# Zeros on PE before the first inputs, v scaled on GpSimd ahead of its loads, and k of three batches turned by DMA transposes

One core of a Trainium2 chip. The metric is the device time of one execution in microseconds (us), median over the runs; most runs of one kernel lie within 0.3% to 1% of each other. A run over 1.5% above the fastest of its kernel counts as slow here, and only fast runs are compared.

## The reference

Two stages. A block-wise linear attention with decay over q, k, v of 4 batches x 8 heads x 768 positions x 64; then a token mixer whose input x is the attention's output.

```python
# attention, per head, blocks of 64: rel = i - j
intra = (qb @ kb.T * where(rel >= 0, lam ** rel, 0)) @ vb
inter = (qb * lam ** (pos + 1)) @ kv_state
kv_state = lam ** 64 * kv_state + (kb * lam ** (63 - pos)).T @ vb
out = intra + inter
# mixer, per batch
W = (x @ w_q) @ (x @ w_k).T / sqrt(64)
y = relu(W @ x) @ w_out
```

## The kernel before

PE is the engine for matmuls, DVE the one for vectors, ACT the one for activations, GpSimd (POOL in the views) a general one; SyncE (SP) issues transfers. SBUF is the memory on the chip that they work from, HBM the large one outside it. k turned is kT, v scaled is vn.

The kernel walks over 16 pairs of heads (4 batches x 4 pairs, numbered 0 to 15), with chunks of 128 positions. The decay is folded into q (multiplied by `Dq`) and into v (multiplied by `DvI`). All inputs are float32 in HBM and are cast to bf16 by loads that GpSimd issues, five pairs ahead. For a pair, PE turns q and k (transposes against an identity), makes the scores, the states (`dps`) and the output (`oa`); DVE masks the scores; ACT copies kT and the output. The mixer's matmuls of the batch before are woven between (`pq`, `py`, `pm`, `po`). The instructions of each engine run in program order. The code is shortened; `NP` is 4 (pairs in a batch), `N` 16, and `...` stands for what is left out.

```python
def load_kv(n):                                    # GpSimd: one issue for k, one for v
    for nm, src in (("k", k), ("v", v)):
        t = stage.tile([128, 2, NCH, D], BF16, tag="f" + nm, name="f" + nm)
        nc.gpsimd.dma_start(out=t, in_=kv_rows(n, src))

def turn(n):
    ...                                            # 12 transposes of q, qT on DVE
    trk = pst([128, S], BF16, "trk")
    for c in range(NCH):
        for hl in range(2):
            nc.tensor.transpose(trk[hl*64 : hl*64+64, c*CH : (c+1)*CH], kn[:, hl, c, :], ident)
    nc.scalar.copy(out=kT, in_=trk)

for n in range(N):
    if n + AHEAD < N:
        load(n + AHEAD)                            # q, k, v of pair n + 5
    if n == 0:
        load_wo()
    if n + 2 < N:
        take_k(n + 2)
        if n + 2 >= NP:
            scale_v(n + 2, nc.gpsimd)              # vn = v * DvI, pairs 4 to 15
    scores(n)
    ...                                            # mixer parts of the batch before
    inter(n)
    if n + 2 < NP:
        scale_v(n + 2, nc.vector)                  # pairs 2 and 3
    values(n)
    states(n + 1)                                  # needs vn of pair n + 1
    turn(n + 2)
```

## Time and profile before

| | before |
|---|---|
| time | 109.6 us (109.4 to 109.9) |
| span in the profile | 108.0 us |
| PE, GpSimd, DVE, ACT busy | 88.6, 65.5, 69.3, 65.2 us |
| loads: last packet | 71.6 us |
| loads while undisturbed | some 160 GB/s of bf16, 3.6 us a pair |

The busy shares say that PE is the fullest engine, but they are an average.

One row misleads, as the prediction notes: the page's clock row of this kernel is 9 throughout. The trace's first clock record of this run is at 20.0 us; until then the page shows full speed.

### The profile page before, as it was taken

The page shows a single profiled execution, that of the slowest core. Times are in us where ns is not written, and L with a number is a line of the kernel's source. Part 1 is how long each engine was busy: PE and PEld are TensorE (multiplying, and loading weights), DVE is VectorE, ACT ScalarE, POOL GpSimd, SP SyncE. Part 2 cuts the span into 40 slices and gives each one's busy share as a digit, 9 for nine tenths or more (in the row PEclk, how much of TensorE's full clock was granted, in tenths as well). Part 3 has the DMA queues.
Part 4 walks back from the last instruction along what each step waited for, and adds up shares of the span by engine and source line. Part 5 has one row for each costly group of instructions (what it writes and reads, how often), then busy time and mean ns, then how long its engine had stood idle before and what let it go on. Part 6 is the DMA issues. An engine that isn't in the chain of part 4 may idle for free. (4 is left out here: it accounts for less than half of the span.)

```text
span 108.0 us, 3286 instructions
## 1 busy us (share of the span) xinstructions
PE 88.6 (82%) x1392; PEld 58.7 (54%) x1392; DVE 69.3 (64%) x168; ACT 65.2 (60%) x119; POOL 65.5 (61%) x68
## 2 busy tenths in 40 slices
PE   0013979977796998899999999999999999998950
PEld 0013849666474766657686557487675645543410
DVE  1435597999975979772988918458988190227440
ACT  4036194845547268678665969696488777647420
POOL 5999999849979999999999999232000000000000
PEclk9999999999999999999999999999999999999999
DMA  0999999999999999999999999990000435522383
GB/s 17 187 168 164 165 162 161 167 164 170 197 164 168 163 162 164 164 167 189 251 210 166 166 166 213 263 283 11 6 0 0 178 119 194 194 97 103 142 323 118
DMA packets 67406, 16.93 MB, mean 157 GB/s; under 512 B 63808, under 2 KB 64320, under 8 KB 67392
## 3 DMA queue, kind: packets, MB, share of 16 engines
q0 software_dynamic: 61184, 9.77, 121.6%
q1 hardware_dynamic: 6208, 6.95, 19.3%
q8 instruction: 11, 0.18, 0.6%
q14 instruction: 3, 0.02, 0.1%
HBM read 20.19 MB, written 6.29 MB: 245 GB/s over the span
## 5 line engine op out<-in xcount | busy, mean ns | idle before, releaser
L282 DVE TENSOR_TENSOR pr<-sc,maskc 128x384 bf16<-128x384 f32 x64 | 31.1, 550 | 0.6
L423 PE MATMUL po<-wo,rmT 128*128 128x512 bf16 x96 | 22.3, 379 | 0.0
L322 ACT CAST xT<-oa 128x384 bf16<-128x384 f32 x32 | 17.3, 594 | 5.9 <-PE oa L314 5.1
L193 POOL TENSOR_TENSOR vn<-fv,DvI 128x768 bf16<-128x768 bf16 x12 | 17.8, 1498 | 3.8 <-PE trk L223 3.8
L227 ACT COPY kT<-trk 128x768 bf16<-128x768 bf16 x16 | 12.8, 799 | 10.6 <-PE trk L223 10.2
L434 ACT COPY osb<-po 128x512 f32<-128x512 f32 x21 | 12.3, 586 | 8.8 <-PE po L423 7.2
L77 POOL DMA_DIRECT2D fk<-in_k_dram x15 | 15.8, 1056 | 2.3 <-DMA fq<-in_q_dram 1.6
L77 POOL DMA_DIRECT2D fv<-in_v_dram x15 | 15.6, 1039 | 0.4 <-DMA fq<-in_q_dram 0.3
L208 PE MATMUL trq<-ident,fq 128*64 128x128 bf16 x192 | 9.3, 237 | 7.6 <-DMA fq<-in_q_dram 7.6
L71 POOL DMA_DIRECT2D fq<-in_q_dram x16 | 14.1, 883 | 1.1 <-POOLq L519 0.8
L423 PEld LDWEIGHTS <-rmT 128*128 128x128 bf16 x96 | 9.1, 98 | 9.9 <-DVE rmT L407 0.5
L250 DVE COPY two<-dps 128x64 f32<-128x64 f32 x16 | 3.6, 224 | 16.6 <-PE dps L240 16.6
L314 PE MATMUL oa<-pr,vn 128*64 128x128 bf16 x192 | 10.9, 228 | 2.6 <-DVE pr L282 2.2
L335 DVE COPY xnat<-xp 128x768 bf16<-128x768 bf16 x16 | 8.8, 550 | 4.9 <-PE xp L334 4.9
L270 PE MATMUL sc<-qT,kT 64*128 64x128 bf16 x192 | 10.8, 228 | 0.9 <-ACT kT L227 0.5
L416 ACT ACTIVATE rmT<-pm 128x384 bf16<-128x384 f32 x28 | 11.5, 507 | 0.0
L208 PEld LDWEIGHTS <-fq 128*64 128x64 bf16 x192 | 7.0, 121 | 7.6 <-DMA fq<-in_q_dram 7.6
L214 DVE TENSOR_TENSOR qT<-trq,dq 128x768 bf16<-128x768 bf16 x16 | 8.8, 550 | 2.4 <-PE trq L208 2.4
L314 PEld LDWEIGHTS <-vn 128*64 128x64 bf16 x192 | 7.0, 111 | 5.5 <-issue 4.1
L270 PEld LDWEIGHTS <-kT 64*128 64x128 bf16 x192 | 7.1, 99 | 4.2 <-issue 2.1
L334 PE MATMUL xp<-ident,xT 128*128 128x128 bf16 x96 | 8.4, 225 | 0.3
L223 PE MATMUL trk<-ident,fk 128*64 128x128 bf16 x180 | 8.4, 232 | 0.1
(53 smaller groups left out, 107.3 us busy)
## 6 DMA issues: line engine op xcount, KB each, us to landing
out_dram<-osb SPq DMA_DIRECT2D x24, 256.0 KB, 2.2
fq<-in_q_dram POOLq DMA_DIRECT2D x16, 192.0 KB, 7.5
fv<-in_v_dram POOLq DMA_DIRECT2D x16, 192.0 KB, 8.5
fk<-in_k_dram POOLq DMA_DIRECT2D x15, 192.0 KB, 8.0
wo<-in_moe_w_out_dram POOLq DMA_DIRECT2D x1, 512.0 KB, 11.0
k<-in_k_dram SPq DMA_DIRECT2D x1, 384.0 KB, 3.9
wqk_f<-in_moe_w_q_dram SPq DMA_DIRECT2D x1, 128.0 KB, 5.9
wqk_f<-in_moe_w_k_dram SPq DMA_DIRECT2D x1, 128.0 KB, 7.2
```

What stands on the lines that cost most here:

```text
L71: nc.gpsimd.dma_start(out=t, in_=q_rows(n))
L77: nc.gpsimd.dma_start(out=t, in_=kv_rows(n, src))
L193: eng.tensor_tensor(out=vn, in0=fv, in1=DvI[:, 2 * kk : 2 * kk + 2, :].unsqueeze(3).to_broadcast([128, 2, NCH, D]), op=ALU.mult,)
L208: nc.tensor.transpose(trq[hl * 64 : hl * 64 + 64, a, r, :], fq[:, hl, a, r * D : (r + 1) * D], ident,)
L227: nc.scalar.copy(out=kT, in_=trk)
L270: nc.tensor.matmul(sc[a, hl][:, cc, :], kT[r, c * CH : (c + 1) * CH], qchunk(n, r, c), start=True, stop=True, skip_group_check=True,)
L282: nc.vector.tensor_tensor(out=t, in0=sc[a, hl], in1=maskc, op=ALU.mult)
L314: nc.tensor.matmul(oa[a][r, cc, :], vn[:, hl, c, :], pr[a, hl][:, cc, :], start=False, stop=(cc == 2), skip_group_check=True,)
L322: nc.scalar.copy(out=xT[b][:, kk, a * HALF : (a + 1) * HALF].rearrange("d (c p r) -> d c r p", c=3, r=2), in_=oa[a].rearrange("d c (r p) - ...
L416: nc.scalar.activation(out=to, in_=pms[dd, n], func=ACT.Relu, scale=1.0 / 8.0)
L423: nc.tensor.matmul(po, M[b]["rmT"][:, kt, t * CH : (t + 1) * CH], wo[:, kt, :], start=(kt == 0), stop=(kt == 3),)
L434: nc.scalar.copy(out=osb, in_=po)
```

## The change

Intent: warm PE's clock while it waits for q; stop PE's waits for v by scaling it ahead of the loads in GpSimd's order, and take two more v and four copies off DVE; take 144 transposes off PE and twelve copies off ACT, by letting the DMA engines turn k. The diff is shortened.

```diff
+WARM = 11
 def load_kv(n):
-    for nm, src in (("k", k), ("v", v)):
-        t = stage.tile([128, 2, NCH, D], BF16, tag="f" + nm, name="f" + nm)
-        nc.gpsimd.dma_start(out=t, in_=kv_rows(n, src))
+    t = stage.tile([128, NCH, 2, D], BF16, tag="fk", name="fk")
+    for hl in range(2):
+        nc.gpsimd.dma_start(out=k_rows(t)[:, hl], in_=kv_rows(n, k)[:, hl])
+    t = stage.tile([128, 2, NCH, D], BF16, tag="fv", name="fv")
+    nc.gpsimd.dma_start(out=t, in_=kv_rows(n, v))
 def turn(n):
+    if n >= NP:
+        return                                     # after q's part
+def turn_k(n):
+    kT = tsb.tile([128, S], BF16, tag="kT", name="kT")
+    nc.sync.dma_start_transpose(
+        out=kT.rearrange("d (c p) -> d c p", p=128),
+        in_=L[n]["kn"].rearrange("p c h d -> p (c h d)"),
+    )
 def flip(n):                                       # the xnat copy
+    if b == 0: nc.scalar.copy(...)                 # else nc.vector, as before
+for _ in range(WARM):
+    nc.tensor.matmul(warm, blank[:, 0:128], blank, start=True, stop=True)
 for n in range(N):
+    if n + 2 < N:
+        take_k(n + 2)
+        if n + 2 >= NP:
+            turn_k(n + 2)
+        scale_v(n + 2, nc.gpsimd)                  # pairs 2 to 15
     if n + AHEAD < N:
         load(n + AHEAD)
-    if n + 2 < N: ... scale_v(n + 2, nc.gpsimd)    # was here; pairs 2, 3 on nc.vector below
```

A DMA transpose of a pair wants k with both heads side by side in each chunk. A load that writes this pattern in one issue does not build, so each k load becomes two.

More of the change, by code (lines that the diff above doesn't have):

```diff
@@ L67, in kv_rows, with k_rows @@
         return src[b, 2 * kk : 2 * kk + 2].rearrange("h (c p) d -> p h c d", p=128)
+    def k_rows(t):
+        return t.rearrange("p c h d -> p h c d")
     def load_q(n):
@@ L74, in load_kv @@
     def load_kv(n):
-        for nm, src in (("k", k), ("v", v)):
-            t = stage.tile([128, 2, NCH, D], BF16, tag="f" + nm, name="f" + nm)
-            nc.gpsimd.dma_start(out=t, in_=kv_rows(n, src))
-            staged[n, nm] = t
+        t = stage.tile([128, NCH, 2, D], BF16, tag="fk", name="fk")
+        for hl in range(2):
+            nc.gpsimd.dma_start(out=k_rows(t)[:, hl], in_=kv_rows(n, k)[:, hl])
+        staged[n, "k"] = t
+        t = stage.tile([128, 2, NCH, D], BF16, tag="fv", name="fv")
+        nc.gpsimd.dma_start(out=t, in_=kv_rows(n, v))
+        staged[n, "v"] = t
     def load(n):
@@ L98 @@
     nc.scalar.preload_act_table_set("natural_log_exp_and_others")
+    blank = consts.tile([128, HD], BF16, name="blank")
+    nc.vector.memset(blank, 0.0)
     ident = consts.tile([128, 128], BF16, name="ident")
@@ L182, in take_k @@
         if n == 0:
-            kn = nat.tile([128, 2, NCH, D], BF16, tag="kn", name="kn")
-            nc.vector.tensor_copy(out=kn, in_=k0)
+            kn = nat.tile([128, NCH, 2, D], BF16, tag="kn", name="kn")
+            nc.vector.tensor_copy(out=k_rows(kn), in_=k0)
         else:
@@ L219, in turn @@
         )
+        if n >= NP:
+            L[n].update(qT=qT)
+            return
         trk = pst([128, S], BF16, "trk")
@@ L223, in turn @@
                 nc.tensor.transpose(
-                    trk[hl * 64 : hl * 64 + 64, c * CH : (c + 1) * CH], kn[:, hl, c, :], ident
+                    trk[hl * 64 : hl * 64 + 64, c * CH : (c + 1) * CH], kn[:, c, hl, :], ident
                 )
@@ L228, in turn @@
         L[n].update(qT=qT, kT=kT)
+    def turn_k(n):
[4 more added lines that the diff above has]
+        )
+        L[n]["kT"] = kT
     def qchunk(n, r, c):
@@ L241, in states @@
                     dps[hl * 64 : hl * 64 + 64, c:end, :],
-                    kn[:, hl, c, :],
+                    kn[:, c, hl, :],
                     vn[:, hl, c, :].unsqueeze(1).to_broadcast([128, end - c, D]),
@@ L334, in flip @@
             nc.tensor.transpose(xp[:, t, :], xT[b][:, kk, t * CH : (t + 1) * CH], ident)
-        nc.vector.tensor_copy(out=xnat[b][:, :, kk * CH : (kk + 1) * CH], in_=xp)
+        to = xnat[b][:, :, kk * CH : (kk + 1) * CH]
+        if b == 0:
+            nc.scalar.copy(out=to, in_=xp)
+        else:
+            nc.vector.tensor_copy(out=to, in_=xp)
     M = {}
@@ L435, in mix_po @@
         nc.sync.dma_start(out=out[b, t * CH : (t + 1) * CH, :], in_=osb)
+    warm = pst([128, HD], F32, "warm")
+    for _ in range(WARM):
+        nc.tensor.matmul(warm, blank[:, 0:128], blank, start=True, stop=True)
     make_dq(0)
@@ L456 @@
             load_wo()
-        if n + 2 < N:
-            take_k(n + 2)
-            if n + 2 >= NP:
-                scale_v(n + 2, nc.gpsimd)
         scores(n)
@@ L479 @@
         inter(n)
-        if n + 2 < NP:
-            scale_v(n + 2, nc.vector)
         values(n)
```

## The prediction

> **What bounds the kernel now.** I read the page's busy shares and slices first, then the instructions in order of time on each engine, then the table of waits, then the chain that ended last.
>
> ```profile
> PE   0013979977796998899999999999999999998950
> DVE  1435597999975979772988918458988190227440
> ACT  4036194845547268678665969696488777647420
> POOL 5999999849979999999999999232000000000000
> DMA  0999999999999999999999999990000435522383
> ```
>
> A slice is 2.7 us. PE is full from about 43 us to the end. GpSimd is full nearly from the start to about 67 us, and the DMA engines are full to about 72 us. So there are two regimes: until about 45 us loads and GpSimd pace PE, afterwards PE paces itself. The page's chain (PE 15%, all of it after 86.9 us) speaks only for the tail, so I take the middle from the order of time.
>
> ```profile
> 48.00 0.89 POOL L71 DMA_DIRECT2D fq<-in_q_dram  x1
> 48.88 1.03 POOL L77 DMA_DIRECT2D fk<-in_k_dram  x1
> 49.88 1.05 POOL L77 DMA_DIRECT2D fv<-in_v_dram  x1
> 50.91 1.51 POOL L193 TENSOR_TENSOR vn<-fv,DvI 128x768 bf16<-128x768 bf16 x1
> 52.33 0.89 POOL L71 DMA_DIRECT2D fq<-in_q_dram  x1
> ```
>
> This is one pair of heads on GpSimd (columns: start, duration, both us): 4.33 us from one q issue to the next, back to back. GpSimd has no room here. It stays ahead of PE only because a PE iteration in batches 2 and 3 takes about 5 us (scores of pair 8 at 51.11, of pair 12 at 71.92: 20.8 us for four).
>
> ```profile
> DVE two L250 <- PE dps L240: 16.6, 14, 2.6
> ACT kT L227 <- PE trk L223: 10.2, 10, 2.3
> PE trq L208 <- DMA fq<-in_q_dram: 7.6, 1, 7.6
> PE oa L314 <- DVE pr L282: 2.2, 8, 0.5
> PE dps L240 <- DVE vn L193: 1.7, 1, 1.7
> PE dps L240 <- POOL vn L193: 1.6, 3, 0.9
> ```
>
> Of these waits only those of PE cost time. PE starts at 7.65 us because q of pair 0 lands then. In batch 1 its state matmuls (dps) already wait for v scaled on GpSimd.
>
> ```profile
> L193 POOL TENSOR_TENSOR vn<-fv,DvI 128x768 bf16<-128x768 bf16 x12 | 17.8, 1498 | 3.8 <-PE trk L223 3.8
> L77 POOL DMA_DIRECT2D fk<-in_k_dram x15 | 15.8, 1056 | 2.3 <-DMA fq<-in_q_dram 1.6 <-DMA wo<-in_moe_w_out_dram 0.7
> L71 POOL DMA_DIRECT2D fq<-in_q_dram x16 | 14.1, 883 | 1.1 <-POOLq L519 0.8 <-DMA fv<-in_v_dram 0.3
> L227 ACT COPY kT<-trk 128x768 bf16<-128x768 bf16 x16 | 12.8, 799 | 10.6 <-PE trk L223 10.2
> L193 DVE TENSOR_TENSOR vn<-fv,DvI 128x768 bf16<-128x768 bf16 x4 | 3.8, 957 | 2.0 <-DMA fv<-in_v_dram 2.0
> L175 POOL DMA_DIRECT2D wo<-in_moe_w_out_dram x1 | 0.8, 812 | 0.0
> ```
>
> These are the rows that the change touches or that its cost is worked out from.
>
> **What the Trainium skill says.** "TensorE: Matmul & The Clock Gate", Part 1: PE's clock is halved until some 3.4 us of sustained work. The trace agrees in kind: twelve transposes span 0.85 us at 7.65 us and 0.53 us at 21.37 us, and the change comes only at 20.3 us. (The clock row of the page shows 9 throughout and doesn't show this.) "DMA: Bandwidth & Descriptors", section "SWDGE vs HWDGE vs iDMA": GpSimd's cores compute the descriptors of the loads it issues; the section "Anatomy of one DMA — SWDGE (gpsimd) path" calls the generation small and variable. The trace shows it is not small here: 0.81 to 1.05 us of GpSimd per issue. The same page, "Latency and other measured facts", gives 261 GB/s for a DMA transpose with a non-contiguous middle dimension. No run before this one shows a DMA transpose. "GPSIMD Engine Reference", section 3.1, has GpSimd 1.96 times as long as DVE for a two-input operation; here it is 1498 ns to 957 ns, 1.57.
>
> **The change part by part.**
>
> *Zeros on PE.* Eleven matmuls of 512 columns. At half speed, an estimate of 11 x 0.43 = 4.7 us from the skill's page (512 columns at 1.2 GHz), from about 1.4 us to 6.1 us, before q lands at 7.65: they cost nothing. If they warm PE, its groups between 7.65 and 20.3 us shrink as 0.85 to 0.53. It is busy 1.49 + 3.73 + 4.60 = 9.8 us in the three stretches of 5 us from 5 to 20 us, so that is worth 3.7 us at most. But turn(1) waits for loads up to 12.24 us and the state matmuls of pair 2 will wait for GpSimd (below), so I count close to nothing.
>
> *k turned by DMA.* It removes 12 x 12 = 144 transposes. One group holds PE for about 0.44 us (75.45 to 75.88 us), 12 x 0.44 = 5.3 us in all; and 12 copies on ACT of 0.80, 9.6 us, mostly not on the path. In its place are 12 transposes of 192 KB on SyncE's queue; an estimate with the skill's 261 GB/s is 0.75 us of DMA each. k is loaded about three iterations ahead, some 15 us, so their latency is hidden unless they take far longer than that.
>
> *k loaded in two halves.* The layout that the transpose wants makes each k load two issues of 768 runs in place of one of 1536. What is an issue worth? w_out, 128x4 = 512 runs, 0.812 us; q, 768 runs, 0.883; k, 1536 runs, 1.056. That is nearly a line, about 0.72 + 0.22 ns a run, and doesn't follow the bytes. So a half costs about 0.87, and a pair gains 2 x 0.87 - 1.03 = 0.7 us on GpSimd, 15 x 0.7 = 10.6 us in all.
>
> *v on GpSimd.* Pairs 2 and 3 move from DVE (0.96) to GpSimd (1.42 from start to start): 2.8 us more there, 1.9 us less on DVE. Four xnat copies move from DVE (0.55) to ACT. DVE was full at 20 to 25 us, so batch 0 would be relieved, if DVE stayed its bound.
>
> *Sum on GpSimd.* 65.5 + 10.6 + 2.8 = 78.9 us, in program order, and the order matters: the scaling of pair 13 now stands behind the last load. Step by step: load 1 from 4.70, about 3.9 (its k issue was slow); mask 0.5; loads 2 to 4 at 0.85 + 2 x 0.85 + 1.01 = 3.56 each, to 19.8. Then scale 2 to 21.2 (before: DVE at 17.0 to 18.0), load 5 to 24.8, w_out to 25.6, scale 3 to 27.0, load 6 to 30.6. Then nine rounds of 1.42 + 0.88 + 2 x 0.87 + 1.02 = 5.06 us, 45.6, to 76.2; scale 13 to 77.6 us.
>
> PE's states of pair 4 can start at 32.0 us instead of 29.84, and of pair 13 at 77.6 instead of 74.86. Between them PE needs 45.0 - 1.6 (its GpSimd waits) - 9 x 0.44 = 39.5 us against GpSimd's 45.6: GpSimd paces the whole middle, and PE's savings there turn into waiting. From pair 13's states PE runs free: 108.0 - 74.86 = 33.1, less two k groups 0.9, less a little from ACT's freed copies 0.3, is 31.9 us. End at 109.5 us of span; with the 1.64 us between span and time (109.64 - 108.0), 111.1 us.
>
> **The rivals.**
>
> *PE stays the bound.* All PE savings count: 5.3 us of k and up to 3.7 us of the start, about 101 to 104 us. For it: PE is full in the second half, and whoever moves work off PE aims at this. Against it: the 4.33 us of GpSimd per pair are back to back, and the split adds to them. It needs a half issue of 0.70 us or less: one of these issues comes 30 times before pair 13's scaling, so 0.1 us less gives 3 us. Nothing in the three measured sizes suggests so little.
>
> *The DMA engines become the bound.* They were full to 72 us at some 165 GB/s of bf16 (3.6 us a pair). With GpSimd at 5.06 us per pair they get 1.5 us of room per pair, for a transpose and the outputs. At 0.75 us a transpose fits. At 2 us or more, loads fall behind about 1 us a pair, up to 10 us; then 114 to 120 us. For it: 2-byte transposes in small pieces beside small-run loads; the skill's figure is for bandwidth in another kernel. Against it: k and v have two to three iterations of slack.
>
> *The start gains.* A warm PE and a lighter DVE save 3 to 4 us in batch 0 and GpSimd catches up behind. Against it: vn of pair 2 is now behind four loads on GpSimd, so PE has nothing to run earlier.
>
> **Range and chances.** GpSimd's chain gives about 111; 0.05 us on a half issue is 1.5 us either way, waits between queues can only add, and slow transposes give the upper tail. A cheaper issue than I think gives the lower. I say 111.2 us, 107.5 to 116 eight times in ten. The border of "slower" (111.8) is close above my sum and that of "faster" (107.4) needs GpSimd to be 4 us shorter: faster 0.18, same 0.43, slower 0.39.
>
> **What would show it.** Right: GpSimd busy around 79 us in total and back to back until about 76 us; about 5.0 us from one q issue to the next; half k issues of 0.83 to 0.90 us; in the waits, PE's dps behind GpSimd's vn at the top, 0.5 to 1 us per iteration; scores at nearly 5.1 us an iteration in batches 1 and 2; PE full again only from about 78 us; short groups on PE from 8 us on (0.53), yet scores of pair 2 no earlier than 21 us. Wrong: PE's sc waiting for a transposed kT, or vn waiting for its load (the DMA rival); half issues near 0.7 us, PE full from 35 us on (the PE rival); scores of pair 4 before 29 us (the start's rival).

## The result, and the profile after

122.5 us (121.8 to 124.1), against 109.6 of the same chip: slower by 11.5% (ratio 1.115, 95% interval 1.108 to 1.123). One of its four runs was slow; the median of the three fast ones is 122.0 us. A ratio here is the mean time of a kernel's fast runs over that of the other's fast runs in the same rounds, so not quite the ratio of the medians. The prediction was 111.2 us, 107.5 to 116: wrong.

The slices of the changed kernel (a slice is 3.0 us):

```profile
PE   5934785929687828899957984797995899997970
POOL 6999999999999999892958689994031400000000
PEclk9996799995899985599999999599999999999999
DMA  1999999999999999999999999999999451724174
```

The DMA engines are full to 93 us; before it was 72. PE, which was full from 43 us on, has gaps to 95 us. The last load's packet comes at 93.9 us (before: 71.6). Who waits, on the engines and on SyncE's queue:

```profile
PEld L290 <- DMA kT<-fk: 11.2, 7, 3.0
POOL vn L202 <- DMA fv<-in_v_dram: 10.8, 2, 6.6
PE sc L290 <- DMA kT<-fk: 8.5, 5, 2.6
PE dps L260 <- POOL vn L202: 6.7, 7, 1.8
```

```profile
SPq L244 <- DMA fk<-in_k_dram: 63.1, 14, 19.7
```

PE's scores wait for kT out of a DMA transpose; the transposes wait for k's loads; GpSimd's scaling waits for v's loads. Each of these is a wait for a transfer. Only the waits of PE for vn up to about 42 us are those that the prediction expected. GpSimd, start and duration:

```profile
41.31 0.89 POOL L75 DMA_DIRECT2D fq<-in_q_dram  x1
42.19 1.66 POOL L81 DMA_DIRECT2D fk<-in_k_dram  x2
43.80 1.05 POOL L84 DMA_DIRECT2D fv<-in_v_dram  x1
44.83 1.52 POOL L202 TENSOR_TENSOR vn<-fv,DvI 128x768 bf16<-128x768 bf16 x1
46.25 0.89 POOL L75 DMA_DIRECT2D fq<-in_q_dram  x1
...
80.57 1.52 POOL L202 TENSOR_TENSOR vn<-fv,DvI 128x768 bf16<-128x768 bf16 x1
88.67 1.47 POOL L202 TENSOR_TENSOR vn<-fv,DvI 128x768 bf16<-128x768 bf16 x1 [6.58 <-DMA fv<-in_v_dram]
94.34 1.47 POOL L202 TENSOR_TENSOR vn<-fv,DvI 128x768 bf16<-128x768 bf16 x1 [4.20 <-DMA fv<-in_v_dram]
```

Up to 48 us this is the predicted chain: 4.94 us a pair (predicted 5.06), 0.83 us a half k issue (0.87; over all thirty the page has a mean of 0.86), states of pair 4 at 31.6 us (32.0). Then it changes: v of pair 14 was issued by 75.6 us and is scaled at 88.7, v of pair 15 by 80.6 and 94.3. GpSimd now waits where it was expected to set the pace. The queues that the transposes use, before and after (packets, MB, share of 16 engines), and the transposes' own row:

```profile
q1 hardware_dynamic: 6208, 6.95, 19.3%
```

```profile
q1 hardware_dynamic: 15808, 9.31, 36.8%
...
kT<-fk SPq DMA_TRANSPOSE x12, 8.3
```

The twelve transposes bring 9216 packets of 256 bytes, 768 each. In the half microseconds in which more than a hundred of them run and no output does (20.5 us in all), the trace counts 380 of these packets a us and 369 load packets a us, 59 GB/s of loads. Beside no such packets, loads run at some 160 GB/s and, with their smallest rows, some 1200 packets a us. So the two kinds share about one to one. That fits what the Trainium skill says ("DMA: Bandwidth & Descriptors", section "Queues, rings and completion order": each engine goes round its queues packet by packet), though a packet there is a group of descriptors, typically 9 to 17 of them, while the trace counts each row. Together they make far fewer packets than the loads alone. Summed over the stretches with transposes and without outputs, the loads miss what 1.6 us of 160 GB/s would bring, per transpose. The last transpose ran alone, after the last load: its 768 packets took 1.1 us (94.6 to 95.7).

One more thing lies in SyncE's program order: output stores stand behind transposes that wait for their k. ACT waits 2.1 us for stores in this run, but PE waits for ACT's output copy only 0.5 us.

### The profile page after: what moved, and what is told of

Read it like the earlier page. It is cut to its first block, busy times and chain, and to the rows that moved or that the text cites. A ratio compares the mean times of both kernels' runs of the same rounds, so it can differ in the third digit from the quotient of the medians.

```text
span 119.7 us, 3072 instructions
## 1 busy us (share of the span) xinstructions
PE 91.9 (77%) x1259; PEld 55.8 (47%) x1259; DVE 67.2 (56%) x163; ACT 58.5 (49%) x111; POOL 77.9 (65%) x85
## 5 line engine op out<-in xcount | busy, mean ns | idle before, releaser
L202 POOL TENSOR_TENSOR vn<-fv,DvI 128x768 bf16<-128x768 bf16 x14 | 21.2, 1516 | 10.8 <-DMA fv<-in_v_dram 10.8
L81 POOL DMA_DIRECT2D fk<-in_k_dram x30 | 25.3, 863 | 0.9 <-DMA fk<-in_k_dram 0.9
L447 PE MATMUL po<-wo,rmT 128*128 128x512 bf16 x96 | 23.1, 388 | 0.0
L84 POOL DMA_DIRECT2D fv<-in_v_dram x15 | 15.8, 1055 | 4.7 <-PE sc L290 2.4
L290 PE MATMUL sc<-qT,kT 64*128 64x128 bf16 x192 | 10.2, 242 | 9.4 <-DMA kT<-fk 8.5
L440 ACT ACTIVATE rmT<-pm 128x384 bf16<-128x384 f32 x28 | 11.5, 497 | 3.4 <-PE pm L419 3.3
L290 PEld LDWEIGHTS <-kT 64*128 64x128 bf16 x192 | 6.6, 105 | 13.5 <-DMA kT<-fk 11.2
L260 PE MATMUL dps<-vn,fk 128*64 128x128 bf16 (+2 forms) x150 | 6.8, 221 | 6.8 <-POOL vn L202 6.7
L260 PEld LDWEIGHTS <-fk 128*64 128x64 bf16 x150 | 6.1, 114 | 7.8 <-issue 7.7
L354 PE MATMUL xp<-ident,xT 128*128 128x128 bf16 x96 | 9.2, 237 | 0.3 <-ACT xT L342 0.2
L359 DVE COPY xnat<-xp 128x768 bf16<-128x768 bf16 x12 | 6.6, 549 | 4.9 <-PE xp L354 4.9
L313 PE MATMUL oa<-qT,gs 64*64 64x128 bf16 x160 | 8.0, 232 | 0.0
```

The source lines that it names most:

```text
L81: nc.gpsimd.dma_start(out=k_rows(t)[:, hl], in_=kv_rows(n, k)[:, hl])
L84: nc.gpsimd.dma_start(out=t, in_=kv_rows(n, v))
L202: eng.tensor_tensor(out=vn, in0=fv, in1=DvI[:, 2 * kk : 2 * kk + 2, :].unsqueeze(3).to_broadcast([128, 2, NCH, D]), op=ALU.mult,)
L260: nc.tensor.matmul(dps[hl * 64 : hl * 64 + 64, c:end, :], kn[:, c, hl, :], vn[:, hl, c, :].unsqueeze(1).to_broadcast([128, end - c, D]), s ...
L290: nc.tensor.matmul(sc[a, hl][:, cc, :], kT[r, c * CH : (c + 1) * CH], qchunk(n, r, c), start=True, stop=True, skip_group_check=True,)
L440: nc.scalar.activation(out=to, in_=pms[dd, n], func=ACT.Relu, scale=1.0 / 8.0)
```

## The experiments

Theory A: the transposes take DMA time from the loads while these are the limit. Theory B: GpSimd's longer chain is the loss. Theory C: PE's clock is; the changed kernel's clock row shows half-speed windows at about 27, 45 and 75 us which the kernel before does not have. Twelve kernels, all with correct results; each was timed in three or five rounds beside the kernel before (109.4 to 109.7 us).

| run | what it is | us | ratio, 95% interval | last load, us |
|---|---|---|---|---|
| e1 | before + zeros | 110.1 | 1.003 (0.997 to 1.009) | 71.5 |
| e2 | changed, PE turns all k | 112.9 | 1.030 (1.024 to 1.036) | 81.0 |
| e3 | before + 12 unused transposes | 121.3 | 1.095 (1.087 to 1.103) | 93.7 * |
| e4 | before + 12 unused copies, 256-byte rows | 115.0 | 1.047 (1.042 to 1.052) | 87.4 |
| e5 | before + transposes alone | 123.4 | 1.125 (1.120 to 1.131) | 95.1 |
| e6 | changed, DMA turns batch 3 only | 111.8 | 1.023 (1.019 to 1.027) | 84.4 |
| e7 | changed + zeros in two waits | 124.0 | 1.121 (1.113 to 1.129) | 94.4 * |
| e8 | before + v ahead, copies on ACT | 107.3 | 0.980 (0.977 to 0.983) | 73.5 |
| e9 | before + 12 unused copies, 1536-byte rows | 111.7 | 1.017 (1.013 to 1.021) | 80.8 |
| e10 | e8 + DMA turns batch 3 | 105.7 | 0.966 (0.963 to 0.969) | 78.0 |
| e11 | e2 with whole k loads | 107.6 | 0.984 (0.980 to 0.988) | 72.0 |
| e12 | e8 + DMA turns batches 2 and 3 | 114.5 | 1.043 (1.039 to 1.047) | 85.9 |

The us column is the median over all runs; the ratio is of fast runs alone. Where slow runs are among them, the median of the fast ones is 120.2 (e3), 123.3 (e5), 122.6 (e7), 111.6 (e9) and 114.4 (e12). Each last load is of the one profiled run. Those with * fell in the slow state (e3: 123.7 us where its fast runs begin at 119.9), so these two are a little late.

### e1_warm: the zeros alone

The eleven matmuls and the blank tile added to the kernel before.

> The kernel before plus the eleven matmuls on zeros alone. Theory A (transposes hold the DMA engines) says nothing of it beyond the start: short groups on PE from 8 us, scores of pair 1 about 1.2 us earlier (18.4 to 17.2), but pairs 1 to 3 paced by DVE and loads, so 108.5 to 109.6 us. Theory C (PE's clock, dropped to half in five windows, is the loss itself) expects the warm start to be worth its full 3.7 us: 106 to 107.

Same as before within noise. The first two groups of transposes of pair 0 do take 0.53 and 0.50 us (half speed before: 0.85), but the next groups, at 11.0 and 12.1 us, are back at 0.88 and 0.85, and full speed comes back only at about 20 us, as before:

```profile
7.32 0.53 PE L211 MATMUL trq<-ident,fq 128*64 128x128 bf16 x12 [1.19 <-DMA fq<-in_q_dram]
7.68 0.50 PE L226 MATMUL trk<-ident,kn 128*64 128x128 bf16 x12
10.55 0.69 PE L243 MATMUL dps<-vn,kn 128*64 128x128 bf16 x10 [2.37 <-DVE vn L196]
11.01 0.88 PE L211 MATMUL trq<-ident,fq 128*64 128x128 bf16 x12
```

PE waits 2.37 us for vn in between, and the speed is gone. My 1.2 us earlier for pair 1 (17.2) did not come: its scores start at 18.3. Zeros buy speed that PE does not keep here. (In the changed kernel's own profile the half speed lasts from 10.1 to 13.5 us only.)

### e2_pe_turns: the transposes undone

```diff
-            if n + 2 >= NP:
-                turn_k(n + 2)
```
and `turn` does k for all pairs.

> The changed kernel with the DMA transposes alone undone: PE turns k of all pairs again; split k loads, v on GpSimd ahead of the loads, zeros and copies on ACT stay. Theory A: loads get their 160 GB/s back, nothing waits for a load after 45 us, and GpSimd's chain of about 5 us a pair is what is left: 110 to 113 us. Theory B (GpSimd's longer chain is the loss): 119 to 123, as with the transposes. Theory C: half-speed windows stay while PE waits for GpSimd, 114 to 118.

112.9 us: of the 12.4 us that the changed kernel lost (fast runs, 122.0), 9.1 are gone without the transposes. Theory A holds, B is left with the rest, 3.3 us. GpSimd's chain runs through undisturbed:

```profile
71.16 0.89 POOL L75 DMA_DIRECT2D fq<-in_q_dram  x1
72.04 1.65 POOL L81 DMA_DIRECT2D fk<-in_k_dram  x2
73.67 1.04 POOL L84 DMA_DIRECT2D fv<-in_v_dram  x1
74.70 3.08 POOL L202 TENSOR_TENSOR vn<-fv,DvI 128x768 bf16<-128x768 bf16 x2
```

The scaling of pair 13 (the first of the two in the last row) ends at about 76.2 us; the prediction had 77.6.

### e3_extra_turns, e4_extra_copies, e9_extra_long_rows: the transfer by itself

Nothing on PE, ACT, DVE or GpSimd changes; SyncE issues one more transfer of 192 KB for each of pairs 4 to 15, whose result nothing reads.

```diff
+    def extra(n):
+        t = tsb.tile([128, S], BF16, tag="extra", name="extra")
+        nc.sync.dma_start_transpose(                                   # e3
+            out=t.rearrange("d (c p) -> d c p", p=128), in_=<k as 128 x 768>)
+        nc.sync.dma_start(out=<6 pieces of 128, rows apart>, in_=...)  # e4
+        nc.sync.dma_start(out=t, in_=<k as 128 x 768>)                 # e9
```

> The kernel before, all as it was (PE turns k), plus twelve DMA transposes of the same size whose result nothing reads. Theory A: each takes about 2 us of the DMA engines from the loads, which ended at 72 us, so the last load lands at about 94 to 97 and the kernel takes 118 to 126 us, although PE, ACT, DVE and GpSimd do exactly what they did. Theories B and C: nothing on their engines changed, 109 to 111.

> The same as the run with extra transposes, but the twelve are plain SBUF to SBUF copies in rows of 256 bytes: the same bytes, the same 768 packets each. Theory A in the form that the transposing holds the engines: copies run at the rate of the loads' packets (1200 a us), 0.65 us each, 8 us in all, last load at about 80 us, which PE's order hides: 109.5 to 112. If any extra 768 packets cost 2 us, transposed or not: 118 to 126.

> As the run with extra copies, the same bytes again, but in 128 rows of 1536 bytes in place of 768 rows of 256. If what a small extra transfer takes from the loads is its number of packets (the 768-packet copies moved the last load from 71.5 to 87.4 us): a sixth of the packets, last load at 74 to 77, 109.3 to 111 us. If it is the bytes: 114 to 116, as with the 256-byte rows.

e3 settles where the loss comes from: the kernel before, with all its own work, is 9.5% slower by the mere presence of the transposes. But what I expected of the copies was wrong in both runs: I had taken the transposing to be the whole cost, then the packet count. The last load moves from 71.6 to 80.8, 87.4 and 93.7 us, that is 9.2, 15.8 and 22.1 us for twelve: some 0.8 us for the bytes alone in long rows, 1.3 with the same bytes in 768 packets, 1.8 when they are also turned. The missing load bytes in the stretches with these packets give 1.3 us a copy (e4) and 1.9 a transpose (e3, slow; 1.6 to 1.7 in the fast profiles of the changed kernel, e5 and e12). e3's last load is late by its slow state, so turning's part rests on the fast runs: e3 takes 5.2 us longer than e4 (120.2 against 115.0), over 0.4 us a transfer. All three parts are real, and none is the whole.

Where more than a hundred of the extra packets run in a half microsecond, turned and plain ones look alike (loads at 61 GB/s beside e3's, 68 beside e4's). In the half microseconds with fewer of them, the loads reach 143 GB/s in e4, but 84 in e3 (slow) and 92 to 115 in the fast profiles of the changed kernel, e5 and e12. Why a 256-byte packet between SBUF addresses costs that much, and what turning adds inside the DMA engine, stays open.

The copies answer one rival: they stand in the same places of SyncE's order as the transposes of e3, and e9 loses 1.7%. So the order alone isn't the loss. e9's 2.1 us are mostly one early wait: PE waits 2.2 us for a scaled v, until 36 us.

### e5_turns_alone: the transposes without the rest

The changed kernel with zeros, v's order and place, and the ACT copies put back as before; the split k loads have to stay.

> The kernel before with the DMA transposes alone, and the layout and half k loads that they need: no zeros, v on DVE for pairs 2 and 3 and behind the loads on GpSimd as before, copies on DVE as before. If the transposes' hold on the DMA engines is the loss by itself (12 x 1.85 us of load time, as in the run with extra transposes, less 5 us of PE work that is gone): 117 to 122 us, last load about 92 to 95. If the loss needs v's new place on GpSimd as well: 111 to 114.

123.4 us, over 1 us more than I expected at most, and the same as the whole change within noise (1.120 to 1.131 against 1.108 to 1.123): the transposes need nothing of the rest but the split loads to do their harm, and in e3 not even these.

### e6_batch3_alone: four transposes in place of twelve

```diff
-        if n >= NP:          # turn
+        if n >= 3 * NP:
-            if n + 2 >= NP:  # turn_k
+            if n + 2 >= 3 * NP:
```

> The changed kernel with only batch 3's four k turned by DMA, the other eight by PE. If each transpose takes about 1.85 us from the loads, the last load lands 4 x 1.85 = 7.4 us later than without any (80 to about 87-88), and most of the loss is gone: 112.5 to 116 us. If the loss is something that comes once as soon as transposes are in use: 119 to 122.

111.8 us, at or slightly under e2, which has none at all, although the last load is 3.4 us later (84.4 to 81.0). So it is no loss that comes once with the first transpose; and four of them are cheaper for the last load than I expected (0.85 us each, not 1.85). One reason is in the trace: the fourth is issued at 83.9 us, and its packets run after the last load. Another is likely but not tested: with GpSimd issuing a pair every 5 us, the loads, at 3.6 us a pair, leave the DMA engines some time to spare.

### e7_zeros_in_waits: PE's clock

```diff
+        if n in (6, 11):
+            more = pst([128, HD], F32, "more")
+            for _ in range(10 if n == 6 else 8):
+                nc.tensor.matmul(more, blank[:, 0:128], blank, start=True, stop=True)
         scores(n)
```

> The changed kernel with ten zero matmuls (2.2 us) before the scores of pair 6 and eight (1.7 us) before those of pair 11, where PE waits 2.6 and 2.1 us for a transposed k: they keep PE busy in the wait, so that its clock shouldn't be halved after it. If the half-speed windows of the middle (3 of 3.4 us) are part of the loss beyond the waits: 118 to 120.5 us. If the loads set the time, PE's clock there is hidden: 121.5 to 124.

The clock row of this run (slow, so its times are not used):

```profile
PEclk9999999995999999999999999999999589999999
```

In it the windows at 45 and 75 us are gone (a later one came), and the time is not better: 1.121 of the kernel before, where the change had 1.115, intervals overlapping. But this run alone doesn't settle theory C: the mean clocks of its two fast runs are 0.901 and 0.915, no higher than the 0.869 to 0.927 of the changed kernel, so it isn't shown that the windows were gone in them too. The clock row of e2, without the transposes, says more:

```profile
PEclk9996555997699999999999999999999999999999
```

By the clock records, PE was at half speed for 13.6 us in e2 and for 17.0 us in the changed kernel (last slice left out; both fast). The 3.4 us more can cost at most 1.7 us of PE's work, and the transposes cost 9.1. Theory C falls as the main cause; two of its three stretches in the middle begin while PE waits for kT (those that end at 45.3 and 75.5 us).

### e8_v_ahead and e11_whole_k: what GpSimd's part is worth

e8 takes two small parts of the change alone: `scale_v(n + 2, nc.gpsimd)` moved ahead of `load(n + AHEAD)` for pairs 4 on, and batch 0's xnat copies on ACT. e11 is e2 with k loaded whole, in the old layout.

> The kernel before with two small parts of the change alone: v scaled on GpSimd ahead of the loads (pairs 4 on; pairs 2 and 3 stay on DVE) and batch 0's xnat copies on ACT. No transposes, no split loads, no zeros. GpSimd's work doesn't grow, so PE's waits for it in batch 1 (1.6 us) and some of DVE's crowding in batch 0 go: 106.5 to 109, and 109 to 110 if the loads pace that stretch anyway.

> The changed kernel without the DMA transposes (112.9 us) and also without the split k loads; zeros, v on GpSimd ahead of the loads for pairs 2 to 15 and the ACT copies stay. If GpSimd's chain of 5.0 us a pair is what made 112.9 out of it, taking 0.65 us a pair off it brings pair 13's scaling from 76 to about 68 us, ahead of PE: 106.5 to 109.5 us. If it is v of pairs 2 and 3 on GpSimd or the zeros: 111 to 113.

Both come to 107 to 108 us. From e2 to e11 only the split k loads go, and with them 5.3 us. So the 3.3 us that e2 left to theory B come from the split, which costs even more than that; the rest of GpSimd's new work costs nothing that shows. v ahead with the ACT copies is a gain of 2.0% by itself (1.7 to 2.3; which of the two brings it was not tested). v of pairs 2 and 3 on GpSimd and the zeros are worth nothing that shows (e11 against e8: 0.984 and 0.980).

### e10_v_ahead_batch3 and e12_v_ahead_from_8: how many transposes pay

On e8, with the split k loads for the turned pairs only (`BY_DMA` = 12 and 8):

```diff
+            if nm == "k" and n >= BY_DMA:      # two half loads, heads side by side
+        if n >= BY_DMA: ... nc.sync.dma_start_transpose(...)   # take_k
+        if n >= BY_DMA: return                                  # turn, after q
```

> The run with v ahead (107.3 us) plus DMA transposes for batch 3's k alone, with the split loads for those four pairs alone. They come when the loads are nearly done (about 55 to 75 us) and nothing of batch 3 is short of time: PE loses 4 x 0.44 = 1.8 us of work after 70 us, where it is the bound: 105 to 106.8 us. If even these four hold up the last loads enough to matter: 107 to 109.

> As the run with v ahead and batch 3's k by DMA, but batches 2 and 3 (eight pairs). The four more transposes run while loads stream: about 1.5 to 1.85 us of load time each, 6 to 7 us, and 2.8 us more on GpSimd. Loads have some 8 us to spare at pair 13. If that is used up: 106 to 109 us, no better than with four; if the transposes cost nothing but their packets: 103.5 to 105.

With four, 105.7 us, the best of all: 3.4% faster than the kernel before. PE loses 1.8 us of work where it is the bound, the last load moves from 73.5 to 78.0 us, and PE waits for kT once, 0.2 us:

```profile
77.19 0.51 PE L289 MATMUL sc<-qT,kT 64*128 64x128 bf16 x12 [0.23 <-DMA kT<-fk]
```

With eight, 114.5 us, worse than I allowed for in either case. The last load is at 85.9 us, 2.0 us later for each of the four more, and PE's row shows where it stood still:

```profile
67.66 0.82 PE L289 MATMUL sc<-qT,kT 64*128 64x128 bf16 x12 [2.61 <-DMA kT<-fk]
...
83.41 0.42 PE L259 MATMUL dps<-vn,fk 128*64 128x128 bf16 x9 [1.45 <-POOL vn L209]
...
85.59 0.51 PE L289 MATMUL sc<-qT,kT 64*128 64x128 bf16 x12 [0.97 <-DMA kT<-fk]
```

There is a border, and it lies where the loads' spare time ends. In the five runs with fast profiles whose last load comes after 84 us, the span ends 25.0 to 26.5 us after it (changed kernel 25.8, e4 25.4, e5 25.6, e6 25.0, e12 26.5): the last pair's share and the tail are all that is left to do then. e10's span ends 25.8 us after its last load too, with PE hardly waiting: it stands at that border, with nothing left to spare.

## Why the prediction was wrong, point by point

- **Zeros: right.** They end before q lands (6.1 us against 7.3) and gain nothing (e1: 1.003). That PE loses the speed again by 11 us was not foreseen, and no run shows a cost of it.
- **Half k issues and GpSimd's sum: right.** 0.83 to 0.86 us where 0.87 was worked out from the line through three issue sizes; 4.94 us a pair where 5.06; states of pair 4 at 31.6 where 32.0; in e2 scaling 13 at 76.2 where 77.6. (That this scaling "now" stands behind the last load is loose: it did before, in the row of three from 63.9 us on; pair 12's is the one that moved.) The split alone is worth 5.3 us (e2 to e11). e2, the change without transposes, took 112.9 us; the sum gives 111.1, or 112.3 with the 0.9 and 0.3 us put back that it took off for k. But GpSimd's pace was taken for that of the changed kernel, and there it held only up to 48 us.
- **"an estimate with the skill's 261 GB/s is 0.75 us of DMA each": the step that failed.** Measured, a transpose took 1.6 to 1.7 us from the loads (1.8 by e3's last load), and even alone its packets took 1.1 us. 0.75 is about what a plain copy in long rows costs (e9: 0.8). I took a bandwidth that a transfer can reach as the time that it takes away from others. These are two figures: where the transposes ran thickest, the loads fell from some 160 to 59 GB/s. So the sentence "At 0.75 us a transpose fits" failed, and with it "GpSimd paces the whole middle": from 48 us on, PE and GpSimd waited for transfers.
- **"k and v have two to three iterations of slack": the argument that let the rival go.** Slack hides a latency, and does not help when each pair adds to a queue. A pair needs 3.6 us of load time, some 1.7 us of transpose and its outputs, on DMA engines that get a new pair every 4.94 us. The slack is used up after a few pairs, and v of pairs 14 and 15 could be scaled only 13 to 14 us after their issue (75.6 to 88.7, 80.6 to 94.3).
- **The rival named it, and was too small.** "At 2 us or more ... 114 to 120 us": the mechanism was right, but it was given as an upper tail, and even its end was under the 122.5. It let loads fall behind by up to 10 us; against e2 the last load was 12.9 us later.
- **Among the signs, the right one was listed**: PE's scores wait for kT and vn for its load. It is what came.

## What to carry to other kernels

Before moving work to the DMA engines, add up their time per iteration as for any engine, with every transfer at its cost in the traffic that is there, and compare it with the pace of the loop; slack in the schedule covers a late transfer, not a rate that is too high. To price a transfer, add it unused to the kernel as it is and see how far the last load moves. And take the change apart: two of its parts were gains (2.0% for v ahead of the loads with the ACT copies, 3.4% in all with four transposes at the end of the loads), hidden under two that were losses.

## What the Trainium skill lacked or had wrong

- "Advanced Engine Details and Errata", X-Bar Transpose (TRN2), says that transpose DMAs are as fast as regular ones, and "DMA: Bandwidth & Descriptors", "Latency and other measured facts", gives 261 GB/s. Neither says what a transpose takes from other transfers: 192 KB cost the loads beside it 1.6 to 1.7 us, a plain copy in the same 256-byte packets 1.3, in 1536-byte rows 0.8. Alone, at the end of the loads, one landed 2.7 us after its issue, with its packets in 1.1 us (some 180 GB/s; the last copy of e9, in long rows and alone too, took 0.7 us); beside the loads 6.2 to 9.3.
- "DMA: Bandwidth & Descriptors", section "Why small descriptors are slow (HBM only)", says that SBUF to SBUF transfers don't suffer from small packets. Here, beside loads, 256-byte rows moved the last load by 15.8 us for twelve copies, and 1536-byte rows by 9.2. (No run here has the 256-byte copies alone.)
- The same page, section "Anatomy of one DMA — SWDGE (gpsimd) path", calls the descriptor generation on GpSimd small and says that many descriptors pass before the added cost shows. Here an issue took 0.81 us at 512 runs, 0.88 at 768 and 1.06 at 1536, whatever the bytes: little for each run more, but some 0.7 us for each issue, which that table doesn't have. The page's section "Latency and other measured facts" is nearer, with about 1 us to the first byte for this path.
- "TensorE: Matmul & The Clock Gate", Part 1, says that PE falls to half speed after at least one idle window of about 3.4 us. Here a window in which PE still worked for 0.9 us (e1: from 6.5 us, with a wait of 2.4 us across its end) was followed by half speed from 9.9 us. It lasted until 20.1 us in e1, although PE was busy for most of that time, and until 13.5 us in the changed kernel.
